# Reversing the odd half through DRAM instead of through TensorE, and the small vectors on VectorE instead of GpSimd

## The chip, the cores and the metric

The kernel runs on one core of a Trainium2 chip. The metric is the device time of one execution in microseconds. A core has TensorE (PE, with weight loads shown as PEld), VectorE (DVE), ScalarE (ACT), GpSimd (POOL) and SyncE (SP, which here only issues DMAs).

## What is computed

Two operators are applied to one input `x` of 2048 rows and 1024 columns and mixed by a gate per row:

```python
X = jnp.fft.rfft2(x.astype(jnp.float32), axes=(-2, -1))
a = jnp.fft.irfft2(X * (w_r + 1j * w_i), s=(S, D), axes=(-2, -1)).astype(jnp.bfloat16)

dt = jnp.exp(log_dt)
Lam_bar = jnp.exp(dt * Lam)
B_bar = ((Lam_bar - 1.0) / Lam)[:, None] * Bmat
Bu = jnp.einsum("bld,pd->blp", x + 0j, B_bar)
...
    h = Lam_bar[None, :] * h + Bu[:, t, :]
...
b = 2.0 * jnp.einsum("blp,dp->bld", hseq, Cmat).real + x * Dskip[None, None, :]

g = jax.nn.sigmoid((x * gate_w).sum(-1, keepdims=True))
out = g * a + (1 - g) * b
```

S = 2048, D = 1024, and there are 1024 complex states. The first part is a spectral filter, the second a diagonal state space model.

## The kernel before

**The spectral part.** The transform along the 1024 columns is done on folded data. `x` is turned so that columns lie on partitions (`turn_x`, eight 128x128 transposes to a tile of 128 rows; tile `xT`, four chunks c of 512 rows). `halves(c)` folds a chunk: the sum of the upper and lower 512 columns (L496) is folded again into sum and difference (L498), which is the even half of `xpm`. The odd half is the difference of upper and lower columns in two groups of 256 columns (L502), of which the second has to be reversed along the columns, that is along partitions, before it is added to and subtracted from the first (L513). The reversal is two matmuls for a chunk with an exchange matrix `JJ` (an identity written backwards, L459) into PSUM tile `xps` (L509), evicted by ACT into `xr` (L511). Then come: `fd`, the transform along columns (L650 the even, L655 the odd half, 16 tiles j, each needing both halves of all four chunks; one eviction of 1024 columns to a tile, L661); `s1`, the first step along rows with the table `TF_sb` (L670, eviction L673, store to a DRAM scratch L674); a reload in turned order and the second step `s2w` (L761), the product with W (L767), the inverse steps `is1`, `is2`, `idft`, and a store to `ga_dram`. Two columns are special: `load_Wc` loads two columns of W (L693), `fixup_w` multiplies them on PE (L702 to L704, evicted to `Vc` L706), `fixup` uses them later.

**The state space part.** For each of eight blocks of 128 states (`jb`) `bu` multiplies each chunk by B in bfloat16 (L872, 16 matmuls of 512 columns into `psu`, evicted by ACT into `h`, L875). B comes turned by a transposing DMA (`load_BT`, L859, two blocks' room), except for block 0. DVE then rotates by a table (`rot`, L840 to L846), scans over time (L884), and rotates back (`rot_out`). Each block's table (`table`, L619 to L634) is sines and cosines of a ramp on ACT and a product with the small vectors `cr`, `ci`, `ncr` (L629, L630 on ACT; L631, L634 on DVE into `pn`).

**The small vectors.** Eleven quantities of 128x8 are made from the parameters: step, decay and angle on DVE and ACT (L544 to L557: `dt`, `are`, `r_sb`, `tht`, `kk2`, `rr2`, sine `sn2` and cosine `cs2`), 1/|Lambda|^2 on DVE (L559 to L562), and (Lambda_bar - 1) / Lambda times 2 on POOL (L563 to L575, with two vectors `ns2` for the scan's carry, L576 and L577).

**The end.** `yout` multiplies `h` by C in bfloat16 (L931, plus the skip term L938) into `ps_y`, ACT scales it (L946), POOL adds it in DRAM order into `ga` by an accumulating DMA (L947), and the tile is stored.

**What sets the order.** The kernel does not emit its operations in program order. Every helper (`pe`, `act`, `dve`, `pool`, `dma`) records an operation with an engine, a key, a duration, and the items it reads and writes. `Plan.run` then places them one by one: on each engine the operation that can start first goes first, and among those ready the one with the lowest key. The keys are sums of some forty-five constants (`K_T0` and so on). The order on each engine is fixed by that when the program is built; on the chip each engine runs its list in order and waits by semaphores. Buffers are slots in groups: PSUM has four slots of two banks each, `xr` lies in `M_all`, `h` takes the place of the input tile `xn` and later of `xpm`.

The loads at the start are one list on SP's queue: 16 tiles of x and the block 0 of B, the table `G_all` (L449), `TF_sb` (L450, 832 KB), `TK_sb` (L451), the eight loads of W's columns (L693, 2 KB each in runs of two bytes), then B's transposing loads.

```python
def dma(key, us, fn, r=(), w=(), eng="SP", issue=0.38):
    plan.op(eng, key, 0.0, fn, r, w, gap=issue, dma=us)
sv = lambda key, fn, r, w: dve(key, 0.2, fn, r=[(i,) for i in r], w=[(i,) for i in w])
sg = lambda key, fn, r, w: pool(key, 0.7, fn, r=[(i,) for i in r], w=[(i,) for i in w])
```

Of the kernel before, what the change touches and what calls it, by code (L numbers as in the profile page):

```python
# [297 lines left out]
def kernel(  # L298
# [86 lines left out]
    A2 = nc.scalar.activation  # L385
    K_T0 = -22.17
    K_TB = 61.63
    K_D = 1206.47
    K_O = -1656.09
    K_TAB0 = 405.37  # L390
    K_TAB = -79.77
    K_F0 = 60.42
    K_F = 11.71
    K_W0 = -27.89
    K_W = 37.7
    K_WI = -461.38
    K_I0 = -5003.33
    K_I = 60.06
    K_ID = -162.81
    K_CT = 644.51  # L400
    K_FIX = -1360.15
    K_R1 = 3.77
    K_R2 = 2542.1
    K_RS = 59.87
    K_Y = -2627.1
    K_YS = 416.09
    K_H = 381.09
    K_HM = -216.59
    K_XR = 203.68
    K_HP = -36.47  # L410
    K_XP = -528.77
    K_XS = -325.97
    K_TP = -0.86
    K_DM = 640.15
    K_BT = 425.36
    K_UN = 2960.8
    K_WD = -199.17
    K_KA = -0.82
    K_KR = -9.04
    K_YL = 2155.69  # L420
    K_PC = 1405.74
    K_TL = -24.77
    K_TM = -15.8
    K_D1 = 123.47
    K_WC = 261.15
    K_GATE = 660.92
    KX = lambda c: K_XP * (c > 0) + K_XS * max(c - 1, 0)

# [63 lines left out]
    def halves(c):  # L492
        lo, hi = xT[c][:, 0:4, :], xT[c][:, 4:8, :]
        both = tile_of([P, 4, TC], BF16, "both", "su")
        at = slice(TC * c, TC * (c + 1))
        dve(KX(c) + K_H, 1.22, lambda: nc.vector.tensor_add(out=both.t, in0=lo, in1=hi), r=xT_of(c), w=[(both,)])  # L496
        for g, fn in enumerate((nc.vector.tensor_add, nc.vector.tensor_sub)):
            dve(KX(c) + K_H, 0.69, lambda g=g, fn=fn: fn(out=xpm.t[:, 0, 2 * g:2 * g + 2, at], in0=both.t[:, 0:2, :], in1=both.t[:, 2:4, :]),  # L498
                r=[(both,)], w=[(xpm, c, 0, g)])
        xm = lambda g: xpm.t[:, 1, 2 * g:2 * g + 2, at]  # L500
        for g in (1, 0):
            dve(KX(c) + K_HM, 0.69, lambda g=g: nc.vector.tensor_sub(out=xm(g), in0=lo[:, 2 * g:2 * g + 2, :], in1=hi[:, 2 * g:2 * g + 2, :]),  # L502
                r=xT_of(c), w=[(xpm, c, 1, g)])
        xr = tile_of([P, 2, TC], BF16, "xr", "xr")
        xps = psum([P, 2, TC], "xps")

        def f():
            for g in range(2):
                nc.tensor.matmul(xps.t[:, g, :], lhsT=JJ, rhs=xm(1)[:, 1 - g, :], start=True, stop=True)  # L509
        pe(KX(c) + K_HP, 2 * U, f, r=[(xpm, c, 1, 1), ("JJ",)], w=[(xps,)])  # L510
        act(KX(c) + K_HP, 1.02, lambda: nc.scalar.copy(out=xr.t, in_=xps.t), r=[(xps,)], w=[(xr,)])  # L511
        for g, fn in ((1, nc.vector.tensor_add), (0, nc.vector.tensor_sub)):
            dve(KX(c) + K_XR, 0.69, lambda g=g, fn=fn: fn(out=xm(g), in0=xm(0), in1=xr.t), r=[(xr,), (xpm, c, 1, 0)], w=[(xpm, c, 1, g)])  # L513

# [24 lines left out]
    lbr, lbi, nr, t_a, t_b, t_c, t_d, cr, ci, ncr = [
        small(n) for n in ("lbr", "lbi", "nr", "t_a", "t_b", "t_c", "t_d", "cr", "ci", "ncr")]  # L540
    sv = lambda key, fn, r, w: dve(key, 0.2, fn, r=[(i,) for i in r], w=[(i,) for i in w])
    sa = lambda key, fn, r, w, t=None: act(key, 0.22, fn, r=[(i,) for i in r], w=[(i,) for i in w], table=t)
    sg = lambda key, fn, r, w: pool(key, 0.7, fn, r=[(i,) for i in r], w=[(i,) for i in w])
    sa(1, lambda: A2(out=dt, in_=ldt, func=ACT.Exp), ["vecT"], ["dt"], "exp")  # L544
# [13 lines left out]
    cTC, sTC = cs2[:, 1, :], sn2[:, 1, :]  # L558
    sv(4, lambda: V.tensor_mul(out=den, in0=lre, in1=lre), ["vecT"], ["den"])  # L559
    sv(4, lambda: V.tensor_mul(out=den2, in0=lim, in1=lim), ["vecT"], ["den2"])  # L560
    sv(4, lambda: V.tensor_add(out=den, in0=den, in1=den2), ["den", "den2"], ["den"])
    sv(4, lambda: V.reciprocal(out=inv, in_=den), ["den"], ["inv"])  # L562
    sg(4, lambda: G_.tensor_mul(out=lbr, in0=r_sb, in1=cs2[:, 0, :]), ["r", "cs2"], ["lbr"])  # L563
    sg(4, lambda: G_.tensor_mul(out=lbi, in0=r_sb, in1=sn2[:, 0, :]), ["r", "sn2"], ["lbi"])
    sg(4, lambda: G_.tensor_scalar_add(out=nr, in0=lbr, scalar1=-1.0), ["lbr"], ["nr"])
    sg(4, lambda: G_.tensor_scalar_mul(out=inv, in0=inv, scalar1=2.0), ["inv"], ["inv"])
    sg(4, lambda: G_.tensor_mul(out=t_a, in0=nr, in1=lre), ["nr", "vecT"], ["t_a"])
    sg(4, lambda: G_.tensor_mul(out=t_b, in0=lbi, in1=lim), ["lbi", "vecT"], ["t_b"])
    sg(4, lambda: G_.tensor_add(out=cr, in0=t_a, in1=t_b), ["t_a", "t_b"], ["cr"])
    sg(4, lambda: G_.tensor_mul(out=cr, in0=cr, in1=inv), ["cr", "inv"], ["cr"])  # L570
    sg(4, lambda: G_.tensor_mul(out=t_c, in0=lbi, in1=lre), ["lbi", "vecT"], ["t_c"])
    sg(4, lambda: G_.tensor_mul(out=t_d, in0=nr, in1=lim), ["nr", "vecT"], ["t_d"])
    sg(4, lambda: G_.tensor_sub(out=ci, in0=t_c, in1=t_d), ["t_c", "t_d"], ["ci"])
    sg(4, lambda: G_.tensor_mul(out=ci, in0=ci, in1=inv), ["ci", "inv"], ["ci"])
    sg(4, lambda: G_.tensor_scalar_mul(out=ncr, in0=cr, scalar1=-1.0), ["cr"], ["ncr"])  # L575
    sg(5, lambda: G_.tensor_copy(out=ns2[:, :, 1], in_=sTC), ["sn2"], ["ns2b"])  # L576
    sg(5, lambda: G_.tensor_scalar_mul(out=ns2[:, :, 0], in0=sTC, scalar1=-1.0), ["sn2"], ["ns2a"])  # L577

# [211 lines left out]
    def is2(bp, key):  # L790
# [262 lines left out]
```

## Time and profile before

| | us |
|---|---|
| median of 3 runs | 327.17 |
| lowest, highest | 326.19, 328.23 |
| the profiled execution | 326.46 |
| its span (first to last instruction) | 324.6 |

The profile is of one execution, and durations in it are of single instructions. In a timeline row the columns are start (us), duration (us), engine, line, operation, out <- in, shape, and in brackets the idle time of the engine just before and what ended it. Rows with a count merge instructions that follow each other. Instructions of one engine overlap a little: a DVE operation of 0.69 us is followed by the next after some 0.61. A matmul's duration has the modelled end of its pipeline in it; eight matmuls of 512 columns in a row take 1.73 us.

| group | count | mean ns |
|---|---|---|
| psu matmul L872, 512 columns | 498 | 379 |
| xps eviction L511 (ACT) | 4 | 1058 |
| psu eviction L875 (ACT) | 32 | 1044 |
| odd half's second addition L513 (DVE) | 8 | 684 |
| fd eviction L661 into M_all (ACT) | 12 | 1049 |

### The profile page before, as it was taken

What the parts mean: (1) busy time and instruction counts of PE and PEld (TensorE: products, weight loads), DVE (VectorE), ACT (ScalarE), POOL (GpSimd) and SP (SyncE); (2) the same over time, 40 slices, a digit from 0 to 9 for tenths busy, and PEclk for the clock granted to TensorE, in tenths of its full rate; (3) what the DMA queues carried; (4) which work ended last, traced back from release to release, by engine and by line L of the source; (5) the groups of instructions that cost most, each with busy time, mean ns of one, the idle gap of its engine ahead of it and who ended that gap; (6) DMA issues with size and microseconds to landing.
All of it is one profiled execution on the core that took longest, in us unless ns stands there. A gap on an engine that the chain in (4) does not pass through costs nothing.

```text
span 324.6 us, 5143 instructions
## 1 busy us (share of the span) xinstructions
PE 307.5 (95%) x1836; PEld 165.8 (51%) x1869; DVE 284.1 (88%) x439; ACT 204.7 (63%) x280; POOL 36.1 (11%) x47
## 2 busy tenths in 40 slices
PE   5978899999999999999999999999999999999994
PEld 5644665665444444444476566545444444554442
DVE  3999699999999999999899999999999999904114
ACT  3698699999899999989999998304000222131000
POOL 1137300000000000000000000000000444534000
PEclk9999999999999999999999999999999999999999
DMA  7969326997979999985889999770000787896203
GB/s 227 398 156 68 65 98 175 229 223 187 212 194 292 249 294 298 218 225 100 221 195 216 283 243 274 168 269 17 0 0 2 130 179 174 182 175 124 77 0 129
DMA packets 79409, 56.51 MB, mean 174 GB/s; under 512 B 49684, under 2 KB 65428, under 8 KB 79384
## 3 DMA queue, kind: packets, MB, share of 16 engines
q1 hardware_dynamic: 75848, 53.03, 62.8%
q0 software_dynamic: 3456, 3.15, 8.8%
q8 instruction: 14, 0.23, 0.3%
q14 instruction: 11, 0.09, 0.1%
q10 hardware_dynamic: 80, 0.01, 0.0%
HBM read 28.38 MB, written 16.79 MB: 139 GB/s over the span
## 4 chain that ended last, share of the span: by engine, by line
PE 54%; DVE 18%; ACT 16%; DMA 5%; issue 3%; POOL 3%; DVEq 0%; ACTq 0%
PE psu L872 24%; PE ps_y L931 15%; DVE h L884 7%; DMA ga<-y 4%; DVE h L841 3%; ACT h L875 3%; POOL lbr L563 2%; PE ps_id L814 2%; DVE su L840 2%; PE pt L476 2%; DVE h L842 2%; PE ps_fd L650 2%; PE ps_s L670 2%; PE ps_s L761 2%; PE ps_is L780 2%
## 5 line engine op out<-in xcount | busy, mean ns | idle before, releaser
L872 PE MATMUL psu<-xT,BTs 128*128 128x512 bf16 x498 | 115.8, 379 | 2.8 <-ACT G_all L673 0.5
L931 PE MATMUL ps_y<-CT,h 128*128 128x512 bf16 x499 | 112.7, 379 | 1.5 <-ACT y L946 0.8
L872 PEld LDWEIGHTS <-BTs 128*128 128x128 bf16 x512 | 49.6, 98 | 59.1 <-issue 2.7
L931 PEld LDWEIGHTS <-h 128*128 128x128 bf16 x512 | 49.3, 98 | 57.2 <-issue 1.1
L884 DVE TENSOR_TENSOR_SCAN h<-r_sb,carry,h 128x512 bf16<-128x512 f32 x48 | 60.0, 1272 | 0.0
L946 ACT ACTIVATE y<-ps_y,omg 128x512 f32<-128x512 f32 x24 | 15.7, 685 | 69.4 <-PE ps_y L938 32.8
L947 POOL DMA_DIRECT2D ga<-y x24 | 21.3, 1290 | 241.7 <-DVE ga L919 235.7
L875 ACT CAST h<-psu 128x1024 bf16<-128x1024 f32 x32 | 33.3, 1044 | 0.9 <-PE psu L872 0.6
L842 DVE TENSOR_TENSOR h<-h,su 128x1024 bf16<-128x1024 bf16 (+1 forms) x40 | 23.1, 576 | 0.2
L841 DVE TENSOR_TENSOR h<-h,pn 128x1024 bf16<-128x1024 bf16 (+1 forms) x24 | 20.7, 862 | 0.1
L840 DVE TENSOR_TENSOR su<-h,pn 128x1024 bf16<-128x1024 bf16 (+1 forms) x24 | 20.6, 857 | 0.0
L841 DVE TENSOR_TENSOR h<-h,cs 128x2048 bf16<-128x2048 bf16 x16 | 19.6, 1223 | 0.4
L840 DVE TENSOR_TENSOR su<-h,cs 128x2048 bf16<-128x2048 bf16 x16 | 19.3, 1206 | 0.0
L884 DVE TENSOR_TENSOR_SCAN h<-r_sb,h 128x512 bf16<-128x512 f32 x16 | 18.9, 1210 | 0.0
L819 ACT ACTIVATE M_all<-ps_id,gA 128x1024 bf16<-128x1024 f32 x14 | 16.6, 1235 | 2.7 <-PE ps_id L814 2.7
L764 ACT CAST h<-ps_s 128x1024 bf16<-128x1024 f32 x16 | 15.8, 1023 | 0.6 <-remote 0.5
L784 ACT CAST h<-ps_is 128x1024 bf16<-128x1024 f32 x16 | 15.6, 1016 | 0.0
L803 ACT CAST M_all<-ps_is 128x1024 bf16<-128x1024 f32 x14 | 15.3, 1127 | 0.2 <-PE ps_is L799 0.2
L954 DVE SCALAR_TENSOR_TENSOR o<-ps_y,omg,ga 128x1024 bf16<-128x1024 f32 (+1 forms) x5 | 5.3, 1070 | 11.5 <-issue 9.7
L814 PE MATMUL ps_id<-G_all,M_all 128*128 128x256 bf16 x112 | 14.1, 273 | 0.5 <-ACT M_all L803 0.5
L919 DVE TENSOR_TENSOR ga<-G_all 128x512 bf16<-128x512 bf16 x16 | 6.0, 420 | 9.5 <-DMA out_dram<-ga 9.5
L476 PE MATMUL pt<-ident,xn 128*128 128x128 bf16 x128 | 10.0, 242 | 4.0 <-DMA xn<-in_A_x_dram 3.5
(141 smaller groups left out, 413.5 us busy)
## 6 DMA issues: line engine op xcount, KB each, us to landing
xn<-in_A_x_dram SPq DMA_DIRECT2D x16, 256.0 KB, 4.9
h<-turn_scratch SPq DMA_DIRECT2D x16, 256.0 KB, 5.3
turn_scratch<-h SPq DMA_DIRECT2D x16, 256.0 KB, 2.9
ga_scratch<-M_all SPq DMA_DIRECT2D x14, 256.0 KB, 4.3
M_all<-ga_scratch SPq DMA_DIRECT2D x6, 512.0 KB, 4.4
ga<-y POOLq DMA_DIRECT2D x24, 128.0 KB, 5.9
out_dram<-ga SPq DMA_DIRECT2D x12, 256.0 KB, 2.1
turn_scratch<-M_all SPq DMA_DIRECT2D x11, 256.0 KB, 4.9
```

The lines of the kernel that those rows point to most:

```text
L476: nc.tensor.transpose(out=pt.t[:, j8, :], in_=src()[:, P * j8:P * (j8 + 1)], identity=ident)
L764: act(key, 1.01, lambda: nc.scalar.copy(out=X2.t, in_=ps2.t), r=[(ps2,)], w=[(X2,)])
L814: mm(pz.t[:, at, :], lhsT=ZT.t[:, 2 * par + half, c, :], rhs=Gi_sb[:, par, half, c, :], start=(half == 0), stop=(half == 1))
L819: act(key, 1.11, lambda: A2(out=eo.t, in_=pz.t, func=ACT.Copy, scale=gA[:, bp:bp + 1]), r=[(pz, 0), (pz, 1), ("gA",)], w=[(eo,)])
L840: dve(key, w, lambda: nc.vector.tensor_mul(out=sv(), in0=src()[:, ::-1], in1=bc(1)), r=sitem + [titem(1)], w=[(su,)])
L841: dve(key, w, lambda: nc.vector.tensor_mul(out=dst(), in0=src(), in1=bc(0)), r=sitem + [titem(0)], w=ditem)
L842: dve(key, h, lambda: nc.vector.tensor_add(out=dst()[:, 0], in0=dst()[:, 0], in1=sv()[:, 0]), r=[(su,)] + r0, w=r0)
L872: mm(psu.t[:, ri, :], lhsT=BT.t[:, ri, db, :], rhs=xT[c][:, db, :], start=(db == 0), stop=(db == 7))
L875: act(kb[cc] + K_KA, 1.01, lambda cc=cc, psu=psu: nc.scalar.copy(out=g()[:, :, cc, :], in_=psu.t), r=[(psu, 0), (psu, 1)], w=ui(cc) + ([(" ...
L884: dve(kd, 1.25, lambda cc=cc, ri=ri, carry=carry: nc.vector.tensor_tensor_scan(out=g()[:, ri, cc, :], data0=rb, data1=g()[:, ri, cc, :], i ...
L931: mm(psy.t[:, 512 * dh:512 * (dh + 1)], lhsT=hbuf[jb // 4].t[:, jb % 4, ri, P * tb:P * (tb + 1)], rhs=CT[pc].t[:, ri, jb % 2, 512 * dh:512 ...
L947: dma(key - 1, 1.3, lambda cols=cols, y32=y32: nc.gpsimd.dma_start(out=ga.t[:, tb % 2, cols], in_=y32.t, accum_op=ALU.add), r=[(y32,)] + [ ...
```

## The change

The exchange matrix, its eight matmuls and four evictions go. Each chunk's second group is stored from `xpm` into a DRAM scratch `xr_scratch` by SP's queue, 1024 values to a row, and read back by an indirect DMA from POOL's queue with a column of row numbers `back` (127 - p + 128 c), so that partition p receives row 127 - p. The two groups of 256 columns are swapped by reading `xr` backwards in the addition.

The small vectors that POOL made are made on DVE, with real and imaginary part in one instruction of 128x16 where that can be (`lb`, `m1`, `m2`), and their keys have a constant `K_SM` of their own. `TF_sb` and `TK_sb` are loaded after the third and the fourth store, W's columns after the fourth. `fixup_w` is recorded after the loop over `fd` and `s1`, may run once the store of tile 8 is done, and has a key `K_FW`. The duration that the planner is given for `is2` is 0.46 instead of 0.65. All constants of the keys have new values.

```diff
+    xr_dram = dram.tile([NCH * P, 2 * TC], BF16, name="xr_scratch")
...
-    K_T0 = -22.17
+    K_T0 = -85.52
...
+    K_FW = -261.92
+    K_SM = -2995.37
...
-    dma(16.2, 3.2, lambda: nc.sync.dma_start(out=TF_sb.t, in_=cst["TF"]), w=[(TF_sb,)])
-    dma(16.3, 0.8, lambda: nc.sync.dma_start(out=TK_sb, in_=cst["TK"]), w=[("TK",)])
...
-    JJ = cpool.tile([P, P], BF16, name="JJ")
-    dve(0.5, 0.15, lambda: nc.vector.tensor_copy(out=JJ[:, ::-1], in_=ident), r=[("ident",)], w=[("JJ",)])
+    back = cpool.tile([P, NCH], I32, name="back")
+    pool(0.5, 0.4, lambda: nc.gpsimd.iota(back, pattern=[[P, NCH]], base=P - 1, channel_multiplier=-1), w=[("back",)])
...
-        xps = psum([P, 2, TC], "xps")
-
-        def f():
-            for g in range(2):
-                nc.tensor.matmul(xps.t[:, g, :], lhsT=JJ, rhs=xm(1)[:, 1 - g, :], start=True, stop=True)
-        pe(KX(c) + K_HP, 2 * U, f, r=[(xpm, c, 1, 1), ("JJ",)], w=[(xps,)])
-        act(KX(c) + K_HP, 1.02, lambda: nc.scalar.copy(out=xr.t, in_=xps.t), r=[(xps,)], w=[(xr,)])
+        dma(KX(c) + K_HP, 1.0, lambda: nc.sync.dma_start(out=xr_dram[P * c:P * (c + 1)].rearrange("p (g t) -> p g t", g=2), in_=xm(1)), r=[(xpm, c, 1, 1)], w=[("xr", c)])
+        dma(KX(c) + K_HP, 1.6, lambda: nc.gpsimd.indirect_dma_start(
+            out=xr.t.rearrange("p g t -> p (g t)"), out_offset=None, in_=xr_dram, in_offset=bass.IndirectOffsetOnAxis(ap=back[:, c:c + 1], axis=0)),
+            r=[("xr", c), ("back",)], w=[(xr,)], eng="POOL", issue=1.3)
         for g, fn in ((1, nc.vector.tensor_add), (0, nc.vector.tensor_sub)):
-            dve(KX(c) + K_XR, 0.69, lambda g=g, fn=fn: fn(out=xm(g), in0=xm(0), in1=xr.t), r=[(xr,), (xpm, c, 1, 0)], w=[(xpm, c, 1, g)])
+            dve(KX(c) + K_XR, 0.69, lambda g=g, fn=fn: fn(out=xm(g), in0=xm(0), in1=xr.t[:, ::-1]), r=[(xr,), (xpm, c, 1, 0)], w=[(xpm, c, 1, g)])
...
-    sv(4, lambda: V.tensor_mul(out=den, in0=lre, in1=lre), ["vecT"], ["den"])
...
-    sg(4, lambda: G_.tensor_mul(out=lbr, in0=r_sb, in1=cs2[:, 0, :]), ["r", "cs2"], ["lbr"])
...
-    sg(5, lambda: G_.tensor_scalar_mul(out=ns2[:, :, 0], in0=sTC, scalar1=-1.0), ["sn2"], ["ns2a"])
+    lam = vecT[:, 0:2, :]
+    two = lambda v: v[:, None, :].to_broadcast([P, 2, 8])
+    cr, ci = co[:, 0, :], co[:, 1, :]
...
+    sv(4, lambda: V.tensor_mul(out=lb, in0=trig[:, :, 0, :], in1=two(r_sb)), ["r", "cs2", "sn2"], ["lb"])
+    sv(4, lambda: V.tensor_scalar_add(out=lb[:, 0, :], in0=lb[:, 0, :], scalar1=-1.0), ["lb"], ["lb"])
+    sv(4, lambda: V.tensor_mul(out=lb, in0=lb, in1=two(inv)), ["lb", "inv"], ["lb"])
+    sv(4, lambda: V.tensor_mul(out=m1, in0=lb, in1=lam), ["lb", "vecT"], ["m1"])
+    sv(4, lambda: V.tensor_mul(out=m2, in0=lb, in1=lam[:, ::-1, :]), ["lb", "vecT"], ["m2"])
+    sv(4, lambda: V.tensor_add(out=cr, in0=m1[:, 0, :], in1=m1[:, 1, :]), ["m1"], ["cr"])
...
-                    dma(key, 0.7, f, r=[("t1", 2)], w=[("Wc", 4 * i + 2 * odd + e)], issue=0.5)
+                    dma(key, 0.7, f, r=[("xr", 3)], w=[("Wc", 4 * i + 2 * odd + e)], issue=0.5)
...
-        pe(key, 0.6, f, r=[("Wc", n) for n in range(8)] + [(TF_sb,)], w=[(vps,)])
+        pe(key, 0.6, f, r=[("Wc", n) for n in range(8)] + [(TF_sb,), ("t1", 8)], w=[(vps,)])
...
-        pe(key, 0.65, f, r=[(Cq,), (TI_sb,)], w=[(psz,)])
+        pe(key, 0.46, f, r=[(Cq,), (TI_sb,)], w=[(psz,)])
...
+    dma(16.2, 3.2, lambda: nc.sync.dma_start(out=TF_sb.t, in_=cst["TF"]), r=[("xr", 2)], w=[(TF_sb,)])
+    dma(16.3, 0.8, lambda: nc.sync.dma_start(out=TK_sb, in_=cst["TK"]), r=[("xr", 3)], w=[("TK",)])
...
-    fixup_w(60)
...
+    fixup_w(K_FW)
```

In the program that is built, SP's list then runs: x and block 0 of B, `G_all`, the two transposing loads of block 1 of B, the four stores, `TK_sb`, two loads of W's columns, `TF_sb`, the other six. The first of the four indirect transfers waits for all four stores; the others stand right behind it.

More of the change, by code (lines that the diff above doesn't have):

```diff
@@ L385 @@
     A2 = nc.scalar.activation
-    K_T0 = -22.17
[L387 to L426, printed above, removed]
+    K_T0 = -85.52
+    K_TB = 57.34
+    K_D = 1052.71
+    K_O = -3605.37
+    K_TAB0 = -319.45
+    K_TAB = -835.91
+    K_F0 = 94.23
+    K_F = 4.58
+    K_W0 = -11.09
+    K_W = 42.77
+    K_WI = -67.69
+    K_I0 = -8767.8
+    K_I = 126.97
+    K_ID = -582.09
+    K_CT = 927.91
+    K_FIX = -4480.0
+    K_R1 = -482.98
+    K_R2 = 2680.1
+    K_RS = 345.7
+    K_Y = -6460.11
+    K_YS = 506.88
+    K_H = 150.29
+    K_HM = -430.83
+    K_XR = 479.43
+    K_HP = 231.19
+    K_XP = -549.66
+    K_XS = -393.86
+    K_TP = -228.78
+    K_DM = 2261.24
+    K_BT = -11.47
+    K_UN = 2498.52
+    K_WD = -484.92
+    K_KA = 485.27
+    K_KR = 39.22
+    K_YL = 2772.28
+    K_PC = 2169.48
+    K_TL = 132.72
+    K_TM = 233.09
+    K_D1 = -73.65
+    K_WC = 146.03
+    K_FW = -261.92
+    K_SM = -2995.37
+    K_GATE = 656.34
     KX = lambda c: K_XP * (c > 0) + K_XS * max(c - 1, 0)
@@ L533, in small @@
         return cpool.tile([P] + list(shape), FP32, name=n)
-    V, G_ = nc.vector, nc.gpsimd
-    dt, are, r_sb, den, den2, inv = [small(n) for n in ("dt", "are", "r_sb", "den", "den2", "inv")]
-    tht, kk2, rr2, sn2, cs2 = [small(n, (2, 8)) for n in ("tht", "kk2", "rr2", "sn2", "cs2")]
+    V = nc.vector
+    dt, are, r_sb, inv, ncr = [small(n) for n in ("dt", "are", "r_sb", "inv", "ncr")]
+    tht, kk2, rr2, sq, lb, m1, m2, co = [small(n, (2, 8)) for n in ("tht", "kk2", "rr2", "sq", "lb", "m1", "m2", "co")]
+    trig = small("trig", (2, 2, 8))
     ns2 = small("ns2", (8, 2))
[L539 to L543, printed above, removed]
+    cs2, sn2 = trig[:, 0], trig[:, 1]
+    sv = lambda key, fn, r, w: dve(key + K_SM, 0.2, fn, r=[(i,) for i in r], w=[(i,) for i in w])
+    sa = lambda key, fn, r, w, t=None: act(key + K_SM, 0.22, fn, r=[(i,) for i in r], w=[(i,) for i in w], table=t)
     sa(1, lambda: A2(out=dt, in_=ldt, func=ACT.Exp), ["vecT"], ["dt"], "exp")
@@ L558 @@
     cTC, sTC = cs2[:, 1, :], sn2[:, 1, :]
-    sv(4, lambda: V.tensor_mul(out=den, in0=lre, in1=lre), ["vecT"], ["den"])
[L560 to L576, printed above, removed]
@@ L577 @@
-    sg(5, lambda: G_.tensor_scalar_mul(out=ns2[:, :, 0], in0=sTC, scalar1=-1.0), ["sn2"], ["ns2a"])
+    lam = vecT[:, 0:2, :]
+    two = lambda v: v[:, None, :].to_broadcast([P, 2, 8])
+    cr, ci = co[:, 0, :], co[:, 1, :]
+    sv(4, lambda: V.scalar_tensor_tensor(out=sq, in0=lam, scalar=0.5, in1=lam, op0=ALU.mult, op1=ALU.mult), ["vecT"], ["sq"])
+    sv(4, lambda: V.tensor_add(out=inv, in0=sq[:, 0, :], in1=sq[:, 1, :]), ["sq"], ["inv"])
+    sv(4, lambda: V.reciprocal(out=inv, in_=inv), ["inv"], ["inv"])
@@ L580 @@
+    sv(4, lambda: V.tensor_sub(out=ci, in0=m2[:, 1, :], in1=m2[:, 0, :]), ["m2"], ["ci"])
+    sv(4, lambda: V.tensor_scalar_mul(out=ncr, in0=cr, scalar1=-1.0), ["cr"], ["ncr"])
+    sv(5, lambda: V.tensor_copy(out=ns2[:, :, 1], in_=sTC), ["sn2"], ["ns2b"])
+    sv(5, lambda: V.tensor_scalar_mul(out=ns2[:, :, 0], in0=sTC, scalar1=-1.0), ["sn2"], ["ns2a"])
     gB, gA, omg = [cpool.tile([P, 16], FP32, name=n) for n in ("gB", "gA", "omg")]
```

## The prediction

> **What bounds the kernel now.** I read the page first, then a table of busy time by stretch of the span, the timeline of the first 42 us, the chain of waits, and the instructions of single tiles. The engine totals come first.
>
> ```profile
> PE 307.5 (95%) x1836; PEld 165.8 (51%) x1869; DVE 284.1 (88%) x439; ACT 204.7 (63%) x280; POOL 36.1 (11%) x47
> ```
>
> TensorE is close to the bound, and the shares hide a division into stages. The stretch table (length, then busy us of PE, PEld, DVE, ACT and POOL, clock, DMA share, GB/s):
>
> ```profile
> 12.00:16.00 4.00, 3.84 (x46) 2.76 (x44) 3.94 (x10) 1.95 (x3) 0.00 (x0) 1.00 1.06 408
> 16.00:20.00 4.00, 3.20 (x41) 2.51 (x42) 3.88 (x6) 3.97 (x6) 1.34 (x2) 1.00 1.07 329
> 20.00:24.00 4.00, 3.00 (x13) 1.25 (x13) 3.90 (x8) 4.00 (x6) 1.73 (x4) 1.00 0.32 10
> ...
> 32.00:36.00 4.00, 4.00 (x27) 2.63 (x26) 1.54 (x3) 0.47 (x1) 3.21 (x9) 1.00 0.00 0
> 36.00:40.00 4.00, 2.58 (x20) 2.04 (x19) 3.68 (x4) 4.00 (x6) 0.00 (x0) 1.00 0.63 131
> ...
> 41.40:200.00 158.60, 155.88 (x922) 85.22 (x938) 156.73 (x235) 155.04 (x214) 0.00 (x0) 1.00 0.90 221
> 200.00:281.00 81.00, 79.75 (x425) 39.06 (x432) 80.59 (x119) 15.85 (x22) 12.67 (x16) 1.00 0.48 115
> 281.00:319.20 38.20, 37.94 (x215) 19.07 (x219) 11.26 (x24) 5.06 (x8) 8.62 (x10) 1.00 0.54 104
> ```
>
> From 41 to 200 us three engines are at 98%; from 200 to 281 PE and DVE are; after 281 only PE is. So what the first 41 us lose is not made up, and only the opening has idle time. The timeline shows where it goes:
>
> ```profile
> 19.45 0.38 PE L509 MATMUL xps<-xpm,JJ 128*128 128x512 bf16 x1 [0.29 <-ACT xT L479]
> 20.36 0.59 PE L509 MATMUL xps<-xpm,JJ 128*128 128x512 bf16 x2 [0.54 <-ACT xT L479]
> ...
> 26.08 7.52 POOL L563 TENSOR_TENSOR lbr<-r_sb,cs 128x8 f32<-128x8 f32 x1 [4.35 <-ACT cs L557]
> ...
> 32.86 0.68 DVE L513 TENSOR_TENSOR xpm<-xpm,M_all 128x1024 bf16<-128x1024 bf16 x1
> ...
> 35.52 0.73 ACT L629 ACTIVATE tt<-tf,ci 128x512 f32<-128x512 f32 x1 [4.01 <-POOL ci L574]
> 36.29 0.75 DVE L631 SCALAR_TENSOR_TENSOR pn<-tf,cr,tt 128x512 bf16<-128x512 f32 x1 [2.75 <-ACT tt L629]
> 38.72 0.59 PE L670 MATMUL ps_s<-M_all,TF_sb 128*128 128x512 bf16 x2 [1.42 <-ACT M_all L661]
> ```
>
> The exchange matmuls L509 sit in front of the psu matmuls from 19.15 to 22.19 us, waiting for evictions, and a 128x8 product on POOL takes 7.52 us, until DVE first falls idle (32.86 + 0.68 = 33.54; POOL ends at 33.60). Behind it ACT stands 4.0 us, DVE 2.75 us, and the first column transforms L670 wait 1.42 us. Clock was 1.00 throughout.
>
> **The change, part by part.** The sum is made against the profiled execution: 326.46 us, span 324.6; the median of the three runs is 327.17, 0.71 above it.
>
> PE. Removed: 8 matmuls L509, which at the pace of psu (eight in 1.73 us) are 1.7 us. In the changed program PE runs the last transposes, then 96 psu matmuls unbroken, then fd. The transposes end at 19.15 us now; ACT will have the cosine of the vectors (0.38) and four copies instead of three behind its table load, so I put the first of the 96 at 20.0. 96 x 0.2163 = 20.8, so fd begins at 40.8. At 41.46 now, PE has done 64 psu, 32 fd matmuls, 6 of L670 (together 32 x 0.109 + 6 x 0.216 = 4.8 us) and the 0.5 us of L702 to L704. The changed PE then has 48 more psu done (10.4 us), and lacks 4.8 - 0.66 = 4.1 us of fd and L670 and the 0.5: a **lead of 5.7 us**.
>
> ACT. Removed: four evictions L511, 4.2 us. Gone too is the 4.0 us stand. Against the same moment it has done three more evictions of psu and the whole table of state block 1 (9 operations, some 5 us in all), and lacks four copies of fd and L670: a lead of about 4 us.
>
> DVE. Thirteen short operations take the place of POOL's fifteen and of the four around den: nine more, spaced 0.08 to 0.12 us as L545 to L550 are, 1.0 us at most. JJ (0.53) went where DVE waits anyway (2.35 us before its first copy), and the added table of row numbers lies in the same wait on POOL: both nothing. Walked in program order: at 19.02 now DVE has finished its copies; changed, 19.02 + 1.0 - 0.67 (L622 moved behind) = 19.4. The next sum and the differences of chunks 3 and 2 wait for ACT's last copies (21.8) and end at 23.3, the one that the last store needs at 22.7. Ten operations on the even half and block 0's table follow, 7.9 us by their rows: DVE reaches the first addition of the reversed part (L513 now) at 31.2. Four additions more, L622 of block 1, one addition, four rotations (3.5 us), an addition, L631, and the last addition: it ends at 40.9, 1.2 us before PE needs it (40.8 + three even groups, 1.3). The scan then starts at 41.6, against 41.36 now, with three operations of block 1's table (2.0 us) already done: a **lead of 1.8 us**, provided no addition waits.
>
> Store and indirect transfer. Four stores of 256 KB on SP's queue, behind G and the two transposing loads of block 1, ahead of TK, TF and Wc. They replace nothing on that queue; TF (needed by L670 near 44 us) now lies behind two Wc loads, which at 13.2 us for eight issues are 1.65 each, so it still lands near 33. In the built program the first of the four indirect transfers carries the wait for all four stores: they do not run chunk by chunk. The last store is issued at 22.7, and a 256 KB store lands in 2.9 (L785) to 4.9 us (L674). No row shows an indirect transfer. The nearest is the other transfer that POOL issues:
>
> ```profile
> L947 POOL DMA_DIRECT2D ga<-y x24: 859/1211/1912, 251.8 to 296.8; - x24
> ...
> DMA to landing us min/median/max: 3.0/5.9/7.2
> ```
>
> With the last store at 25.6 and 0.9 us per issue, the second transfer, which the first addition needs, starts at 26.5 and lands at 29.5 to 33.7; the store's upper end adds 2. So DVE waits 0 to 4.5 us at 31.2. I take a landing of 4.5, which ends at 31.0, no wait: L947 adds 256 KB into memory in place, which this doesn't, and plain loads of 256 KB (M_all<-turn_scratch) land in 3.5. Nothing else issues on POOL before 250 us. Behind a DVE that waits stand block 0's rotation and scans, and the odd half of fd, so PE.
>
> Whether DVE can hold up POOL's issue is the open cost. By rows: L947 took 3.5 to 3.7 us for four while DVE was 100% busy (251 to 280 us) and 3.5 for four at 295, with DVE mostly idle: a direct issue isn't held. L563, which reads two tiles of SBUF, was held 7.5 us. An indirect issue reads the tile of row numbers. [...]
>
> Wc's work moved from 30.57 (0.89 us of wait) into the fd stretch: its 0.5 us stay. The planner's keys are all different, so everything behind 41 us is reordered too; PE had 2.7 us idle between 41.4 and 200 and 1.3 to 281, so that can return at most 4.0 us, and what it may cost isn't shown. I put it at nothing.
>
> The sum: PE leads by 5.7, ACT by 4, DVE by 1.8. PE alone ends the kernel, and DVE, done at 281, has time behind it; but from 41 to 281 DVE is at 99% and hands PE its h. I take the middle of 1.8 and 5.7, 3.7: 326.46 - 3.7 = 322.8 for the execution, and 327.17 - 3.7 = **323.5 us** for the median.
>
> **Rivals.** *The lead is given back in the fd stretch.* Behind 41 us the changed PE runs eight pairs of fd and L670 almost bare of psu: a pair costs PE 0.87 + 0.43 = 1.31 us and ACT two copies at 0.95 apart, 1.9. Eight pairs leave PE 4.7 us idle of its 5.7, unless four PSUM buffers soften it. For it: ACT is at 98% there now. Against it: ACT arrives 4 us ahead. Time: 327.17 - 1.0 = 326.2.
>
> *The indirect issues are held until DVE runs dry, and the kernel is slower.* DVE has work without a gap from 23.3 to 31.2. If, as L563 did, the first issue ends only then, the second transfer starts at about 32.1 and lands 3.0 to 5.9 us later: DVE stands 3.9 to 6.8 us at L513's successors, 2.1 to 5.0 behind today after its lead. The last addition moves to 44.8 to 47.7, PE stands 2.7 to 5.6 at the odd fd, and loses 0 to all of its 5.7. With DVE the bound to 281, 327.17 + 3.5 = 330.7, to 332 at the upper end. It decides once the second transfer lands behind 33.0 (31.2 + 1.8). Against it: the L947 rows. For it: L563.
>
> **How the numbers follow.** Forecast 0.57: 321.5 (all of PE's lead) to 325.4 (DVE's alone). First rival 0.18. Second 0.20. The remaining 0.05 is a reordering behind 41 us that costs. About 1% (3.3 us) is what a measurement of this kernel tells from no change: faster is below 323.9. Of the forecast 0.41 lies there and 0.16 within 1%; the first rival is within; the second, with 330.7 in its middle, is above 330.4 with 0.12 and within with 0.08; the rest counts as slower. Faster 0.41, same 0.16 + 0.18 + 0.08 = 0.42, slower 0.12 + 0.05 = 0.17. The range goes from 320.8 (PE's whole lead and the 0.7 by which a profiled run can lie under the median) to 331.0, which leaves out the top of the second rival.
>
> **What would show it.** In the changed profile: psu without a break from about 20 to 41 us; no stand of ACT before its table products; indirect issues of about 0.9 to 1.3 us each, the first near 26; DVE's first addition near 31 with no DMA wait, the last near 41; PE idle under 1 us at the odd fd. Wrong would be: an issue on POOL several us long, or DVE waiting at the additions for more than 1.8 us; ACT-released gaps of PE from 45 to 62 us that add up to over 3 us; or a lead that is there at 60 us and gone at 200.

## The result, and the profile after

The changed kernel takes 331.54 us (median of 6 executions, 331.15 to 335.27) against 326.68 us for the kernel before beside it (325.81 to 328.28): a ratio of 1.0159, 95% interval 1.0122 to 1.0196. It is slower by 1.6%, where 323.5 us was forecast. Its profiled execution took 333.57 us, with a span of 331.8.

The engine totals of its page:

```profile
PE 310.8 (94%) x1861; PEld 166.1 (50%) x1861; DVE 284.5 (86%) x447; ACT 200.9 (61%) x276; POOL 27.3 (8%) x37
```

They look like those of before, and again do not say where the time went. (Before's page has 33 fewer matmuls than weight loads, so idle time counted in its rows is an upper bound.) The table by stretch does (length, then busy us of PE, PEld, DVE, ACT, POOL, clock, DMA share, GB/s):

```profile
24.00:28.00 4.00, 4.00 (x21) 1.79 (x19) 3.93 (x7) 3.56 (x6) 1.61 (x2) 1.00 0.97 157
28.00:32.00 4.00, 4.00 (x20) 1.84 (x19) 3.57 (x5) 3.47 (x6) 3.16 (x3) 1.00 1.12 207
32.00:36.00 4.00, 4.00 (x21) 1.80 (x19) 0.00 (x0) 2.04 (x3) 0.00 (x0) 1.00 1.20 185
36.00:40.00 4.00, 4.00 (x20) 1.83 (x19) 3.26 (x6) 0.00 (x0) 0.00 (x0) 1.00 0.69 50
40.00:44.00 4.00, 2.19 (x17) 1.58 (x15) 3.88 (x5) 3.47 (x6) 0.00 (x0) 1.00 1.01 130
44.00:48.00 4.00, 1.56 (x12) 1.22 (x11) 4.00 (x7) 2.93 (x5) 0.00 (x0) 0.93 0.01 1
48.00:60.00 12.00, 11.76 (x69) 7.85 (x67) 11.69 (x18) 11.55 (x14) 0.00 (x0) 0.88 0.48 100
...
80.00:100.00 20.00, 18.14 (x88) 8.04 (x87) 18.23 (x30) 17.24 (x27) 0.00 (x0) 1.00 0.85 242
...
160.00:180.00 20.00, 17.44 (x137) 10.87 (x136) 18.76 (x31) 19.90 (x26) 0.00 (x0) 1.00 0.74 197
```

To 40 us PE never stops, as forecast. VectorE does nothing at all from 32 to 36 us, and some 10 us later PE is idle for 4.2 us (2.19 and 1.56 busy of 4.00 and 4.00). Its clock then falls to 0.88 for the stretch behind. Two places much further on, at 80 and at 160 us, cost PE 1.9 and 2.6 us; before has 0.3 and 1.1 there:

```profile
80.00:100.00 20.00, 19.66 (x94) 8.82 (x95) 20.00 (x33) 18.73 (x29) 0.00 (x0) 1.00 0.82 194
...
160.00:180.00 20.00, 18.92 (x165) 13.38 (x167) 19.93 (x31) 20.00 (x24) 0.00 (x0) 1.00 0.96 224
```

The timeline has the cause of the first loss; the second is taken up with the experiments. A row marked SPq is SP's queue issuing DMAs; the bracket is the idle time before, and what ended it:

```profile
20.21 20.88 PE L866 MATMUL psu<-xT,BTs 128*128 128x512 bf16 x96
...
24.10 1.02 SPq L687 DMA_DIRECT2D Wc<-in_A_w_r_dram  x2
...
26.08 1.04 SPq L687 DMA_DIRECT2D Wc<-in_A_w_r_dram  x2
26.09 1.40 POOL L507 DMA_INDIRECT M_all<-xr_scratch,back  x1 [24.09 <-DMA xr_scratch<-xpm]
...
27.16 10.79 SPq L687 DMA_DIRECT2D Wc<-in_A_w_i_dram  x4
...
27.79 1.00 POOL L507 DMA_INDIRECT M_all<-xr_scratch,back  x1 [0.30 <-issue]
...
36.74 3.10 DVE L511 TENSOR_TENSOR xpm<-xpm,M_all 128x1024 bf16<-128x1024 bf16 x5 [5.17 <-DMA M_all<-xr_scratch,back]
...
40.53 0.64 ACT L618 ACTIVATE tt<-tt 128x512 f32<-128x512 f32 x1 [5.30 <-DVE tt L616]
...
43.77 0.60 PE L644 MATMUL ps_fd<-G_all,xpm 128*128 128x256 bf16 x4 [1.81 <-ACT h L869]
...
46.80 2.27 PE L649 MATMUL ps_fd<-G_all,xpm 128*128 128x256 bf16 x12 [2.44 <-DVE xpm L511]
```

The indirect transfers are issued when they were expected and quickly. The first addition (L511 now) stands 5.17 us for the data of the second. ACT, which needs a product that VectorE makes behind the first additions (L616), stands 5.30 us with it and evicts `psu` late, for which PE waits 1.81 us; PE's odd half (L649) then waits 2.44 us for the last addition. How long the transfers took is the last row of the instructions of L507, from issue to landing:

```profile
DMA to landing us min/median/max: 8.7/9.3/10.3
```

For the second, which landed at 36.7 us, that is 8.9 us, where 4.5 had been taken. Three theories were to be told apart. **A**: the eight loads of two columns of W (`Wc`), which the change put behind the last store, are in the DMA engines at the same time and hold the transfers up. **B**: an indirect transfer takes 9 us by itself. **C**: the new order behind 41 us costs what the transfer saves.

### The profile page after: what moved, and what is told of

It is laid out like the page before. It is cut to its first block, busy times and chain, and to the rows that moved or that the text cites. A ratio compares the mean times of both kernels' runs of the same rounds, so it can differ in the third digit from the quotient of the medians.

```text
span 331.8 us, 5175 instructions
## 1 busy us (share of the span) xinstructions
PE 310.8 (94%) x1861; PEld 166.1 (50%) x1861; DVE 284.5 (86%) x447; ACT 200.9 (61%) x276; POOL 27.3 (8%) x37
## 4 chain that ended last, share of the span: by engine, by line
PE 66%; ACT 10%; DMA 4%; issue 3%; DVE 2%; SPq 2%; DVEq 0%; ACTq 0%
PE ps_y L925 33%; PE psu L866 18%; PE ps_id L808 3%; PE ps_y L932 2%; PE ps_is L775 2%; PE ps_is L774 2%; PE ps_s L755 2%; PE ps_fd L649 2%; DMA Bcol<-turn_scratch 1%; ACT M_all L667 1%; DMA turn_scratch<-G_all 1%; ACT h L869 1%; DMA turn_scratch<-h 1%; PE ps_fd L644 1%; ACT h L778 1%
## 5 line engine op out<-in xcount | busy, mean ns | idle before, releaser
L813 ACT ACTIVATE M_all<-ps_id,gA 128x1024 bf16<-128x1024 f32 x12 | 13.4, 1174 | 1.7 <-PE ps_id L808 1.6
L655 ACT CAST M_all<-ps_fd 128x1024 bf16<-128x1024 f32 x13 | 13.5, 1057 | 0.0
L649 PE MATMUL ps_fd<-G_all,xpm 128*128 128x256 bf16 x64 | 10.6, 299 | 2.4 <-DVE xpm L511 2.4
```

The lines of the kernel that those rows point to most:

```text
L649: mm(pf.t[:, 1, :, g, :], lhsT=xA[:, 1, 2 * g + db, j, :], rhs=G_sb[:, db, 1, 256 * g:256 * (g + 1)], start=(db == 0), stop=(db == 1))
```

## Experiments

All were timed beside the kernel before. Several edits rearrange the finished list of operations just before it is emitted; their diffs show that rearrangement.

**Wc's loads left out.** The eight loads are missing from the list, so the correction of two columns is computed from the zeros that the tile is filled with at the start; all else is the changed kernel.

```diff
+        seq = [(o, m) for o, m in seq if not (o.eng == "SP" and o.w and o.w[0][0] == "Wc")]
```

> The changed kernel with the eight loads of W's two special columns left out (the tile stays zero, so that part of the spectral correction is not computed); every other instruction in the order it had. Theory A, the two-byte runs of these loads occupy the DMA engines while the indirect transfers should land: the transfers land in 3 to 5 us instead of 8.7 to 10.3, DVE's wait at the first addition falls from 5.2 us to under 1.5, and the time falls by 3 to 6 us, to 326 to 328. Theory B, an indirect transfer of 256 KB takes 9 us to land by itself: landing and wait stay, time within 1 us of 331.5. Theory C, the loss is made by the reordering behind 41 us: the wait shrinks but the time stays above 330.

Measured: 327.58 us, ratio 1.0018 (0.9991 to 1.0046). The DMA counts, first of the changed kernel, then of this one:

```profile
DMA packets 80817, 58.61 MB, mean 177 GB/s; under 512 B 49812, under 2 KB 66580, under 8 KB 80792
```

```profile
DMA packets 72497, 58.59 MB, mean 180 GB/s; under 512 B 41492, under 2 KB 58260, under 8 KB 72472
...
q1 hardware_dynamic: 68616, 54.07, 62.6%
```

The eight loads are 8320 packets, a tenth of all, for 0.02 MB: two bytes each. Without them the transfers land 4.2 and 5.8 us after issue (the trace has the landing of the last two alone; their median is 5.0), the first addition starts at 31.65 us after a wait of 0.82, the last at 40.98. A holds and B falls: beside the other traffic of this run an indirect transfer took 4.2 to 5.8 us, not 9.

**Each transfer behind its own store.** Four DRAM tensors take the place of one, so that the first transfer doesn't wait for all stores.

```diff
-    xr_dram = dram.tile([NCH * P, 2 * TC], BF16, name="xr_scratch")
+    xr_dram = [dram.tile([P, 2 * TC], BF16, name=f"xr_scratch{c}") for c in range(NCH)]
```

> The changed kernel with the DRAM scratch as four tensors, so that each indirect transfer waits for its own chunk's store alone; the order of everything else as it was. The first two transfers should be issued near 22 us instead of 26.1 and 27.8. Theory A (the loads of W's columns make the landing slow): issued at 22, mostly ahead of those loads (24.1), the first two land in 4 to 6 us, DVE does not wait for the second, and only the fourth transfer is late; time 326 to 329. Theory B (9 us by itself): they land near 31 to 32, so the wait is also nearly gone and the time falls likewise, but the landing stays at 8.7 or more for all four. Theory C: time above 330.

Measured: 328.07 us, ratio 1.0019 (0.9992 to 1.0046). The first issue comes at 22.06 us in place of 26.09. The landings are still slow beside Wc's loads (5.4, 8.5 and 8.8 us for the second to the fourth), but VectorE waits only 1.02 us. Starting four microseconds earlier repairs as much as removing the competitor.

**Wc's loads behind the next block's transposing loads.** Nothing is left out.

```diff
+        wc = [v for v in seq if v[0].eng == "SP" and v[0].w and v[0].w[0][0] == "Wc"]
+        seq = [v for v in seq if v not in wc]
...
+        seq[bt[3] + 1:bt[3] + 1] = wc
```

> The changed kernel with the eight loads of W's columns moved on SP's queue behind the transposing loads of block 2; all else in its order, nothing left out. Theory A: landing 3 to 6 us, DVE's wait under 1.5 us, time 326 to 329, unless the loads then hold up the stores of the first row step near 52 us, which would give back 1 to 3 us. Theory B: landing 8.7 or more, time 331. Theory C: above 330 with the wait gone.

Measured: 327.32 us, ratio 0.9992 (0.9967 to 1.0016). In its table by stretch the loads can be seen by themselves, and two stretches further on matter below:

```profile
36.00:40.00 4.00, 4.00 (x21) 1.78 (x19) 3.88 (x6) 4.00 (x7) 0.00 (x0) 1.00 1.32 28
40.00:44.00 4.00, 4.00 (x34) 3.57 (x33) 4.00 (x7) 3.03 (x5) 0.00 (x0) 1.00 1.25 2
...
80.00:100.00 20.00, 18.14 (x88) 8.07 (x87) 18.20 (x26) 17.17 (x28) 0.00 (x0) 1.00 0.81 192
...
160.00:180.00 20.00, 16.44 (x155) 11.69 (x153) 19.08 (x31) 20.00 (x24) 0.00 (x0) 1.00 0.87 191
```

From 40 to 44 us the DMA engines have a busy share of 1.25 and move 2 GB/s. With this load elsewhere the last two transfers land in 4.9 and 5.5 us, and the timeline has VectorE waiting 0.42 us:

```profile
31.92 3.10 DVE L524 TENSOR_TENSOR xpm<-xpm,M_all 128x1024 bf16<-128x1024 bf16 x5 [0.42 <-DMA M_all<-xr_scratch,back]
```

So the late transfer cost what lies between the ratios 1.0159 and 0.9992, some 5 us of 327. But with the opening as forecast but for these 0.4 us, the kernel only equals the one before.

**Both repairs.** Four DRAM tensors, and Wc's loads moved as above.

> After with both repairs of the opening: each transfer waits for its own store alone, and Wc's loads lie behind block 2. No VectorE wait at any addition. Since the wait is already only 0.4 us with Wc moved, I expect 327 us, as with that alone: what is lost behind 41 us is not touched. A time below 326 would say that the stagger of the landings matters.

Measured: 327.91 us, ratio 1.0023 (0.9987 to 1.006); landings of 5.1 to 6.1 us (the second to the fourth), no wait at any addition. This run also answers a rival of theory A: where Wc's loads stand in front of it, the load of `TF_sb` (832 KB) is late too, and could be what slows the transfers. With Wc moved it is still issued behind the stores, at 23.98 us, 2.02 us ahead of the first transfer (0.92 us in the changed kernel), and the last two land in 4.9 and 5.5 us; here the transfers are issued from 22.51 to 27.55 us, and no landing that the trace has is above 6.1 us, not 9. With no wait left, the opening is out of the question, and the forecast 323.5 us is missed behind 41 us.

**The small vectors alone.** Before, with POOL's fifteen short operations on VectorE in the same places, one by one and not in pairs as in the change.

```diff
-    V, G_ = nc.vector, nc.gpsimd
+    V, G_ = nc.vector, nc.vector
```

> The kernel before with POOL's fifteen small operations issued on DVE at the same places of the order, nothing else changed: one part of the change alone. If POOL's 7.5 us product is a wait for DVE, ACT's stand of 4.0 us before its table products goes and the opening gains 1 to 3 us: 324 to 326 against 326.7. If the stand was hidden behind other waits, or DVE is the bound and pays 1 us for the fifteen: 326.5 to 328.

Measured: 325.91 us (324.89 to 326.64), ratio 0.9945 (0.9922 to 0.9968). The gain is small but real, and this is the fastest of all kernels here, the changed one and the one before included.

**Exchange matmuls in the changed order.** As with Wc moved, with the matmuls and evictions put back where the stores and transfers stood.

> The order of the kernel with Wc's loads moved behind block 2 (327.3 us), with the exchange matmuls and ACT evictions put back in place of stores and indirect transfers. If the transfer is worth what the prediction summed (1.7 us of PE, 4.2 of ACT, and their stalls in the opening), this takes 329 to 332 us. If that lead is given back in any order, because the kernel behind 41 us is bound by something else, it takes 327 to 328. The price of the reordering behind 41 us is this time less the 325.9 us of the kernel of before with the small vectors on VectorE, which does the same work in the order of before: theory C (the order costs what the transfer saves) expects 3 to 6 us, its rival about 1.

Measured: 337.94 us, ratio 1.029 (1.0218 to 1.0361), outside both expectations. The run doesn't answer what it was made for. That order has the differences of columns late, and PE waits three times 1.1 us for the evictions of the reversed part (`M_all`); the last addition starts at 48.68 us in place of 41.25, and the column transforms at 49.60. It shows only that this order isn't to be had without the transfer.

**Fixup of W late, in the order of before.** The kernel with the small vectors alone, Wc's loads moved behind block 2 and the matmuls that need them into the fd stretch.

> Before with the small vectors on VectorE, Wc's loads moved behind the transposing loads of block 2, and the work that needs Wc moved to the middle of the fd stretch. PE's wait of 0.9 us for Wc in the opening goes: if what the opening saves is kept to the end in the order of before, 325.0 to 325.5 us against 325.9; if it is given back, 325.9 or a little more.

Measured: 326.75 us, ratio 0.9988 (0.9961 to 1.0016). PE's wait for Wc is gone, and nothing is won; beside the kernel it is built on (0.9945) it is rather slower.

**The transfer alone, in the order of before.** The same, with stores and indirect transfers for exchange matmuls and evictions; the additions follow the even half.

> The kernel of the run beside it (e8) with stores and indirect transfers in place of exchange matmuls and evictions, each transfer behind its own store, the eight additions together behind the even half, and nothing else moved. Quiet queues: transfers land in about 5 us, the last by about 33. If the lead of the opening is kept in the order of before (theory C: only the reordering took it), 322 to 324 us. If it is given back whatever the order (the fd stretch is bound by ACT and VectorE), 325 to 326, the same as e8. If VectorE waits at the additions, 326 to 329.

Measured: 331.14 us, ratio 1.0111 (1.0078 to 1.0143): slower by 4.4 us than the run beside it, another miss. The last two transfers land in 3.6 and 4.4 us, and still the odd half is late. Table by stretch, then two PE rows of the timeline:

```profile
32.00:36.00 4.00, 0.00 (x0) 0.00 (x0) 1.85 (x4) 0.45 (x1) 0.00 (x0) 1.00 1.05 195
36.00:40.00 4.00, 1.80 (x9) 1.45 (x10) 3.97 (x7) 0.68 (x1) 0.00 (x0) 0.59 1.02 9
40.00:44.00 4.00, 4.00 (x20) 2.82 (x19) 3.88 (x5) 2.61 (x4) 0.00 (x0) 0.56 1.06 2
```

```profile
31.24 0.60 PE L691 MATMUL ps_fd<-G_all,xpm 128*128 128x256 bf16 x4
...
38.20 1.07 PE L696 MATMUL ps_fd<-G_all,xpm 128*128 128x256 bf16 x4 [6.36 <-DVE xpm L554]
```

PE stands 6.36 us, and then four matmuls take 1.07 us instead of 0.60, at a clock of 0.50 (38 to 42 us). The path from difference to addition is a store, an issue and a landing, and takes over 10 us (the four stores are issued between 20.91 and 23.85, the last transfer landed at about 34.8). VectorE waits 2.12 us of PE's 6.36 for a transfer; the rest of the stand comes from the eight additions themselves, which this run puts together behind the even half. But even with only the last chunk's two additions (0.6 us each) left at the last landing, the odd half would not be there before 36 us, 4 us after PE's last matmul. In the order of before PE has 48 psu matmuls to run meanwhile, too few; the changed order puts 96 there. Transfer and order are one package, then, and the question became what these 48 matmuls, run early, cost later. Theory C took this form: psu matmuls are what PE does while ACT evicts the transforms (they cover the evictions), and those that run early are missing there.

**The order of before, from 41 us on.** As with Wc moved; every key carries both sets of constants, and the planner goes over to the old set at 41 us.

```diff
+                       key=lambda v: ((v[1].key.b if t0 >= TURN else v[1].key.a) if isinstance(v[1].key, Two) else v[1].key, v[1].i))
...
+TURN = 41.0
```

> The kernel with Wc's loads moved behind block 2 (327.3 us), unchanged until the first column transforms at 41 us; behind them the planner chooses by the keys of before, so psu matmuls lie again between the inverse transforms of 160 to 200 us (PE 16.44 of 20 us busy at 160 to 180 in the kernel with Wc moved, 18.92 in before). If the lead of the opening (some 5 us) was lost to the order behind 41 us, this takes 322.5 to 324.5 us. If the fd stretch itself takes the lead back (ACT-bound pairs of fd and L670 bare of psu, the first rival of the prediction), PE is idle by 3 us or more from 41 to 80 us and it takes 326 to 327.5.

Measured: 329.47 us, ratio 1.0059 (1.0038 to 1.008), slower than either expectation. The stretch from 160 to 180 us is mended (PE busy 19.07 of 20), but PE is now idle by 5.8 us from 40 to 80 us, where fd stands bare of psu. The loss moved to the earlier place.

**The same from 110 us on** (TURN = 110.0).

> The same, but the keys of before only from 110 us of the planner's time: the fd stretch and the column solve at 87 us (PE waits 1.9 us there) stay as in the changed kernel, and only the end of the state blocks, 160 to 200 us, gets an order like that of before. If the loss lies at 160 to 200 us alone (3.6 us there against 1.1 in before), 324.5 to 325.5 us; if it lies in the fd stretch and at 80 to 100 us, 327 us as without the edit.

Measured: 330.39 us, ratio 1.0118 (1.0069 to 1.0167). 160 to 180 us is mended here too (19.67), and 140 to 160 (18.55) and 180 to 200 (17.17) pay for it.

**64 psu matmuls ahead in place of 96** (TURN = 32.0).

> As the run with the keys of before from 41 us on (329.5 us), but those keys hold from 32 us of the planner's time: 64 psu matmuls lie ahead of the column transforms in place of 96, and 32 more lie between the transforms. Theory (psu matmuls run early are missed later as cover for the ACT-bound transforms): PE now stands some 5 us at the odd half's transforms, since the additions end near 40 us and PE would want them at 35.4, and loses less from 48 to 80 us (4.3 us idle there in the other run, 2 or less here); the sum is again 327 to 330 us. If cover did not matter, the stall would come on top: 333 us or more.

Measured: 333.27 us, ratio 1.0168 (1.0121 to 1.0216). By the time alone this is the case in which cover did not matter. The trace is mixed: PE stands 6.5 us at the odd half, as with the transfer alone, and its clock is 0.5 from 40 to 48 us; but from 48 to 80 us it is idle only 1.5 us, against 4.3 in the run with 96. The expectation had left the clock out, and the time decides nothing.

**psu matmuls early, and nothing else.** Before with the small vectors on VectorE, exchange matmuls kept; the keys of fd are high until 40 us, so that 40 psu matmuls of the fd stretch go ahead of the first column transforms.

```diff
-    K_F0 = 60.42
+    K_F0 = Two(5000.0, 60.42)
...
+TURN = 40.0
```

> Before with the small vectors on VectorE (325.9 us), exchange matmuls and all, the same order in the opening, but 40 psu matmuls of the fd stretch are put ahead of the first column transforms, as the changed kernel has them; no transfer, no wait for one. PE is busy to 41 us in both. Theory (psu matmuls run early are missed later as cover for the ACT-bound transforms): PE idles behind 41 us by some 3 to 5 us more than the 2.2 us of the kernel with the old order, and the time is 328.5 to 331 us. If their place did not matter, 325.5 to 326.5 us.

Measured: 333.50 us (332.76 to 334.91), ratio 1.0189 (1.0153 to 1.0226), where the kernel that it is built on has 0.9945. PE's busy time by stretch, first of the kernel with the old order (with its opening), then of this one:

```profile
20.00:41.00 21.00, 18.71 (x110) 10.12 (x110) 20.90 (x41) 18.09 (x25) 0.00 (x0) 1.00 0.62 53
...
48.00:80.00 32.00, 32.00 (x186) 19.12 (x184) 31.43 (x45) 31.91 (x40) 0.00 (x0) 1.00 0.82 206
...
41.00:200.00 159.00, 157.07 (x940) 85.29 (x939) 156.81 (x235) 155.16 (x214) 0.00 (x0) 1.00 0.88 224
200.00:281.00 81.00, 80.23 (x440) 39.39 (x439) 80.26 (x120) 14.98 (x21) 13.52 (x16) 1.00 0.47 109
```

```profile
48.00:80.00 32.00, 28.96 (x179) 18.88 (x178) 31.77 (x46) 30.72 (x37) 0.00 (x0) 1.00 0.83 211
...
41.00:200.00 159.00, 153.67 (x910) 83.03 (x908) 156.13 (x232) 152.39 (x208) 0.00 (x0) 1.00 0.85 207
200.00:281.00 81.00, 77.77 (x443) 39.01 (x444) 80.77 (x120) 19.70 (x26) 11.91 (x15) 1.00 0.55 132
```

PE is idle 5.3 us from 41 to 200 us in place of 1.9, and 3.2 in place of 0.8 from there to 281. The timeline shows the form that it takes in the fd stretch, first PE, then ACT:

```profile
52.11 0.59 PE L704 MATMUL ps_s<-M_all,TF_sb 128*128 128x512 bf16 x2
53.03 0.60 PE L684 MATMUL ps_fd<-G_all,xpm 128*128 128x256 bf16 x4 [0.32 <-ACT M_all L707]
53.46 0.60 PE L689 MATMUL ps_fd<-G_all,xpm 128*128 128x256 bf16 x4
53.94 0.59 PE L704 MATMUL ps_s<-M_all,TF_sb 128*128 128x512 bf16 x2
54.86 0.60 PE L684 MATMUL ps_fd<-G_all,xpm 128*128 128x256 bf16 x4 [0.32 <-ACT G_all L707]
```

```profile
52.82 1.07 ACT L695 CAST M_all<-ps_fd 128x1024 bf16<-128x1024 f32 x1
53.73 1.08 ACT L707 CAST G_all<-ps_s 128x1024 bf16<-128x1024 f32 x1
54.63 1.09 ACT L695 CAST G_all<-ps_fd 128x1024 bf16<-128x1024 f32 x1
```

One pair of fd and first row step takes 1.83 us (53.03 to 54.86), which is two ACT copies at 0.91 us from start to start; PE has about 1.3 us of work for it and is idle for the other 0.5, of which 0.32 in one piece before fd. With a psu group between the pairs that time is used. From 41 to 80 us PE is idle 3.0 us, all of it waiting for ACT, and the kernel with the old order is idle for none. Here 40 psu matmuls changed places, the opening had no new wait, and the time is 7.6 us longer (333.50 against 325.91). The 3.0 us in the fd stretch are waits for ACT which psu groups fill in the other kernel. From 200 to 281 us the waits are mixed (for ACT, for reloads from DRAM, for VectorE), and the planner chose the rest of the order anew from 40 us, so what part of the 7.6 is that choice isn't known.

## Why the prediction was wrong

**Up to 26 us every step held.** psu ran unbroken from 20.21 (20.0 forecast) to fd at 40.93 (40.8). VectorE was free for the first addition at 31.6 (31.2), and the first indirect issue came at 26.09 ("near 26").

**The step that failed first is the landing**, "I take a landing of 4.5, which ends at 31.0, no wait". It was 8.9 us for the second transfer, which landed at 36.7, and the wait was 5.17 us instead of none. A smaller part is the issue: 0.9 us was taken for the first, and it took 1.40 and 0.30 more to the next, so the second started at 27.79 and not at 26.5. Of the 5.7 us by which it landed late, 4.4 are the landing and 1.3 the issue. With the landing at 5 us (without Wc's loads, or with them moved) the wait is 0.4 to 0.8, and the second transfer is there 4.2 to 4.6 us after its issue, so 4.5 was right for quiet queues. What had been overlooked is the transfers' company. The prediction noted that Wc's loads now lie behind the stores, and asked only whether TF, queued behind two of them, comes in time (it did: issued at 25.17, 7.3 us to land, 32.5 against 33). It did not ask what 8320 two-byte packets do to another queue in the same 10 us. Before's trace had shown them: 13.2 us for eight issues of 2 KB each. The range's upper end of 7.2 us, from L947, was too low as well (and L947's transfers are of 128 KB by the page, not 256).

**That "everything behind 41 us is reordered too" was put "at nothing"**: this is the second failed step, and it is independent of the first: with the landing mended the kernel takes 327.3 us and not 323.5. PE's lead of 5.7 us was counted as psu matmuls done early less transforms not yet done. That is right as a count of work, but these matmuls were cover for ACT's evictions. With Wc moved PE is idle 0 us from 20 to 41 us and 7.8 from 41 to 200; the kernel with the small vectors alone has 2.3 and 1.9. The rows of the kernel with Wc moved:

```profile
20.00:41.00 21.00, 21.00 (x104) 9.73 (x101) 20.38 (x29) 16.53 (x24) 4.79 (x4) 1.00 0.95 182
...
41.00:200.00 159.00, 151.23 (x923) 82.98 (x921) 154.77 (x232) 148.48 (x198) 0.00 (x0) 1.00 0.91 216
```

So "what the first 41 us lose is not made up" was read as if what they gain were kept, and it was not. That psu run early are missed by PE in the fd stretch is shown by the last experiment (3.0 us there, all behind ACT). That the lost lead is wholly this cover isn't shown, and at one place it is something else, as the next paragraph says: three other orders behind 41 us only moved the idle time or added to it, and whether some order keeps the lead stays open.

**The first rival** (lead given back to ACT-bound transforms, 326.2 us) thus names the mechanism of a part of the second half. With Wc moved PE is idle some 4.7 us more from 41 to 200 us than in before (7.8 against 3.1 at most), which is the rival's figure, but by chance: it was summed for the fd stretch alone, and only 2.1 us fall from 40 to 80 us. Most falls at 160 to 180 us, where the inverse transforms stand bare of psu (PE 16.44 of 20, ACT 20.00; 2.7 us of the waits are for ACT, 0.9 for a reload), and 1.9 at 80 to 100, where PE waits for no eviction but for the reload of the special columns:

```profile
86.73 0.19 PE L726 MATMUL zps<-Bcol,TF_sb 128*128 128x31 bf16 x1 [1.86 <-DMA Bcol<-turn_scratch]
```

Before runs the same matmul at 85.21 us without a wait. PE has psu until 84.9 us here and until 85.2 there, so cover isn't what differs: before issues the reload at 80.53 us, 2.3 us behind the last store in front of it, and the kernel with Wc moved at 81.83, 4.0 us behind it. Why the way through DRAM is slower here was not examined.

**The second rival** came closest in time (330.7 to 332), and its turning point, a second transfer behind 33.0 us, is what decided. Its reason is refuted, so that its time was right is luck. The issues took 0.95 to 1.44 us each while VectorE was busy 3.93 and 3.57 of 4.00 us; no issue was held as L563 had been for 7.5. With the transfer alone the first took 2.23 us, the others 0.95 to 1.27. What held L563, and why the issues were not held, though each reads the tile of row numbers, no run here shows.

**The small parts.** Taking the vectors off POOL is worth 1.3 us by itself (327.22 to 325.91), out of the 4 us that ACT stood behind it. The wait of PE for Wc in the opening (0.89 us in before) goes when the matmuls are moved, and nothing is won by it (326.75 us).

## What to carry to other kernels

When a transfer takes the place of work on an engine, look at what else is in the DMA engines in those microseconds, by packets and not by bytes, and at who has to wait through its whole length of store, issue and landing. Work pulled forward to fill that wait is not a lead if it was the filler of a later stretch that another engine bounds: count it there first. And time the parts one by one: here the modest half of the change (small vectors off GpSimd) gives 0.55%, and the ambitious half as it was built takes 2% away (0.5% once Wc's loads are moved).

## What the runs showed of the hardware that was not expected

**Two-byte packets.** With Wc moved, the eight loads of 2 KB had the 16 DMA engines at a share of 1.25 from 40 to 44 us while 2 GB/s moved. In the changed kernel four of their issues took SP's queue 10.79 us, and the transfers issued by POOL took nearly twice as long to land (median 9.3 us for four, against 5.0 without the loads).

**The clock after a stand.** With the transfer alone PE stood from 31.8 to 38.2 us. Its clock was still 1.00 from 32 to 36 us, 0.67 from 36 to 38, and 1.00 again only from 44, 5.8 us after PE had gone back to work:

```profile
32.00:38.00 6.00, 0.00 (x0) 0.00 (x0) 3.81 (x7) 0.45 (x1) 0.00 (x0) 0.89 0.92 135
38.00:42.00 4.00, 3.80 (x18) 3.03 (x19) 3.88 (x6) 1.99 (x2) 0.00 (x0) 0.50 1.16 2
42.00:44.00 2.00, 2.00 (x11) 1.23 (x10) 2.00 (x3) 1.30 (x3) 0.00 (x0) 0.62 1.18 2
44.00:46.00 2.00, 2.00 (x13) 1.16 (x11) 2.00 (x3) 2.00 (x3) 0.00 (x0) 1.00 0.21 57
```

Half speed for 4 us and 0.62 for 2 more lose some 2.8 us (4 x 0.50 + 2 x 0.38), on top of 6.4 us of standing. The profiled execution of the changed kernel has the same from 46 to 52 us (0.86, 0.50, 0.79: 1.7 us lost) after a stretch in which PE was busy 2.75 of 7 us; two others of its executions had a mean clock of 1.000 and still took 331.46 and 331.62 us. Shorter stands had both outcomes: with the exchange matmuls in the changed order PE waited 1.10 us twice (to 28.96 and to 30.65 us), and its clock was 0.84 from 30 to 32 us, 0.50 to 34 and 0.81 to 36; with Wc moved it waited 1.86 us at 86.73, and its clock was 1.00 from 80 to 100. What decides between them no run here shows. A forecast for this kernel that has PE stand over 6 us should add some 2.8 us, an estimate from the run with the transfer alone.
